# Half of a mixing step folded around the last two weighings, copies and casts moved: a fused attention and low-rank mixer on one NeuronCore

## The chip, the cores and the metric

The kernel runs on one core of a Trainium2 chip. A core has five engines that run their own instruction streams and wait for one another through semaphores: TensorE (PE in the profile, PEld for its weight loads), VectorE (DVE), ScalarE (ACT), GpSimd (POOL) and SyncE (SP). SP here only issues transfers, and POOL and ACT issue some too; sixteen DMA engines carry all of them. The metric is the device time of one execution in microseconds. It was 379.27 us before the change (median of three runs, 377.88 to 379.71).

## The reference

Eight batches (B), eight heads (H), 576 positions (S), head size 64 (D). For each batch and head

```
scores = q k^T / 8 + min(-(cum_i - cum_j), 0)      (j <= i; cum = running sum of max(s, 0))
attn   = softmax(scores) v                          -> x, 576 x 512 per batch
u      = x + (x^T U V)^T                            (U 576 x 32, V 32 x 576: mixing over positions)
out    = u + relu(u W1) W2                          (W1 512 x 2048, W2 2048 x 512)
```

All inputs and the output are float32; inside, the matrix products take bf16.

## The kernel before

**Attention.** A head's scores are computed transposed, key by query, without the masked blocks, in four parts of 448, 448, 448 and 256 columns. `scores` issues each part's matmuls into one of three PSUM banks (tag "s") and ScalarE's exponential (line 323) carries it to a tile `pT`; GpSimd masks the diagonal blocks (`affine_select`, line 338). The bias over `cum` is not added: it rides in four extra rows of q and k, so that the product contains it. `weigh` then multiplies `pT` by v with a column of ones (fifteen matmuls, line 367), and VectorE takes the reciprocal and scales the result into `x_sb`.

**Where q and k come from.** For batches 0 to 2, q and k are read with six positions in a partition (`load_six`, into the space of `hT`) and turned by TensorE (`turn_six`): six transposes into a bank, then copies to `kT` and `qT` (line 303) by VectorE, or ScalarE for some. For batches 3 to 7, `cast(b)` has GpSimd issue two DMAs that convert k and q to bf16 in DRAM (`kq_rows`, line 152); later `turn_batch` has SyncE issue, for each of four head pairs, a transposing DMA of k and one of q (`turn_kq`, line 171), and behind the next pair's two transposes the bias rows of the pair before (`bias_rows`, line 278, from `aug_rows`). SyncE's queue is strictly in program order: a transfer that takes long to issue holds all that follow.

**V.** `fetch_v` has SyncE fetch five tiles of v as float32 into `vf`, and `cast_v` has GpSimd convert them into `v_raw` (line 197). For the first batch these stand in the prologue, two tiles (2 and 3) behind four small copies of bias rows.

**Mixing and layers.** Batches go in pairs (a group). The first batch alone is mixed by `mix_first`, in two halves of 256 columns: a sum over position tiles with `U_cat` (line 438), a copy to `ux0` (ScalarE for the first half, VectorE for the second, line 448), then four parts that add `V_cat`'s product to a transposed x (lines 458, 462) and are copied to `uT` (line 465). `layer1` (line 545, ReLU on ScalarE in line 552) and `layer2` (line 564) follow; `beside` interleaves one group's layers on TensorE with the next group's attention and mixing by written costs, in an order that is fixed when the program is built. So each engine runs a fixed sequence, and an engine that waits holds everything behind it. From the second group on, the mixed x goes to `uT` by transposing DMAs from SyncE (line 520).

**Around the change.** `first_attention` runs batch 0 alone. Between its score parts it places the turns of later head pairs (dictionary `turns`, keyed by head and part) and the weighings of earlier heads (`weighed`); after the loop the last three weighings, the two halves of `mix_first` and the turns of the second batch's first pair follow. `fill` matmuls of zeros stand between score parts. U and V are copied to `U_cat` and `V_cat` by GpSimd in the prologue (`place_UV`, lines 136 to 143). From batch 2 on, `ahead_of(c)` runs at the end of each head of batch c:

```python
if h == (6 if c == 2 else 5) and c + 2 < B and c != 3:
    cast(c + 2)
if 5 <= h and c + 1 < B:
    for t in ((0,), (1, 2), (3, 4))[h - 5]:
        cast_v(c + 1, t)
```

Of the kernel before, what the change touches and what calls it, by code (L numbers as in the profile page):

```python
# [40 lines left out]
def kernel(  # L41
# [92 lines left out]
    def place_UV(bi, engine=nc.gpsimd):  # L134
        r, h = slice(R * bi, R * bi + R), slice(64 * bi, 64 * bi + 64)
        engine.tensor_copy(U_cat[:, 5 * bi : 5 * bi + 4, r], U_f[:, :4])
        engine.tensor_copy(U_cat[h, TAIL, r], U_f[h, 4])

        for r0 in (R * bi, 64 + R * bi):
            rows = slice(r0, r0 + R)  # L140
            V_rows = V_cat[rows].rearrange("r t c -> r (t c)")
            if bi == 0:
                engine.tensor_copy(V_rows[:, :S], V_f[rows])
            else:
                engine.tensor_copy(V_rows[:, 640:], V_f[rows, :512])
                engine.tensor_copy(V_rows[:, 576:640], V_f[rows, 512:])
# [135 lines left out]
    def turn_six(b, hp, which, scalar=0, tag="pv", by_head=False):  # L282
        pb = bank(tag, 2 if tag == "pv" else 3).bitcast(BF16)
        for hh in range(2):
            for t in range(SUB // 2):
                c = RP * (hh * (SUB // 2) + t)
                nc.tensor.transpose(  # L287
                    pb[:, c : c + RP],
                    six[min(b, 1)][which][:, 2 * hp + hh, 2 * D * t : 2 * D * t + 2 * D],
                    identity[:RP, :RP],  # L290
                )
# [4 lines left out]
        for e in range(2):  # L296
            from_ = pb[64 * e : 64 * e + 64, : RP * SUB].rearrange(
                "d (h t p) -> d h p t", h=2, p=RP
            )
            for hs in (slice(0, 1), slice(1, 2)) if by_head else (slice(0, 2),):  # L300
                copies.append((hs, e, from_))
        for hs, e, from_ in sorted(copies, key=lambda one: one[0].start):
            (nc.scalar.copy if e < scalar else nc.vector.tensor_copy)(  # L303
                to[:, hs, :, :, e], from_[:, hs]
            )
# [342 lines left out]
    place_UV(0)  # L648
# [15 lines left out]
    for t in (4, 0, 1):  # L664
        fetch_v(0, t)
    for r in range(AUG):
        direct_rows(0, HP - 1, HP, r)
    for t in (2, 3):
        fetch_v(0, t)
    later = cumulate(2, B, nc.gpsimd)  # L670

    def first_attention():
        turn_six(0, 0, 0)
        turn_six(0, 0, 1, scalar=2)
        ps = bank("s", 3)
# [7 lines left out]
        nc.vector.memset(v_raw[0][:, :, :, D : D + 1], 1.0)  # L683
        for i in (0, 1):
            nc.vector.memset(v_raw[0][:64, TAIL + 5 * i], 0.0)
        clear(ones, 1.0)
        clear(zeros, 0.0)
        nc.sync.dma_start(
            out=kA[1][D : D + 1].rearrange("r n (h s) -> r (n h) s", h=2), in_=ones[:H]
        )  # L690
        for r in range(1, AUG):
            nc.sync.dma_start(
                out=qA[1][D + r : D + r + 1].rearrange("r n (h s) -> r (n h) s", h=2), in_=ones[:H]
            )
        for r in range(AUG):
            direct_rows(1, 0, HP, r)
        load_UV(1)
        nc.sync.dma_start(out=kq[:, :, PAIR:].rearrange("i n c -> (i n) c"), in_=zeros)
        nc.sync.dma_start(
            out=aug[1:4].rearrange("r n s -> n r s"),  # L700
            in_=ones.unsqueeze(1).to_broadcast([BH, 3, S]),
        )
# [44 lines left out]
    def second_at_head(h):  # L747
# [3 lines left out]
        if h == 2:  # L751
            place_UV(1)
# [51 lines left out]
    def ahead_of(c):  # L804


        def at_head(h):
# [6 lines left out]
            if h == (6 if c == 2 else 5) and c + 2 < B and c != 3:  # L814
# [61 lines left out]
```

## Time and profile before

| | |
|---|---|
| median of three runs | 379.27 us (377.88 to 379.71) |
| the profiled execution | 380.7 us, of which 379.0 us from its first to its last instruction |
| mean granted clock of TensorE | 0.990 |
| busy: PE, ACT, DVE, POOL | 364.1, 212.6, 137.9, 108.8 us |
| first batch's exponentials | 10.0 to 24.5 us |
| first matmul of the first layer | 30.46 us |

A row of a timeline gives the start in us from the first instruction, the length in us, the engine (a trailing q marks its queue: an issued transfer), the source line, the operation, output<-input, shapes, and a count; in brackets the engine's idle time before it and what ended that. A row of the chain of waits has start, length and the work. DMA rows in a timeline are the issue, not the transfer. Durations on a line with a count are the whole group's.

### The profile page before, as it was taken

How to read it: one execution, taken by the hardware profiler on the slowest of the kernel's cores; microseconds unless marked ns; L12 is line 12 of the kernel's file. 1: busy time of each engine (PE TensorE's matmuls, PEld its weight loads, DVE VectorE, ACT ScalarE, POOL GpSimd, SP SyncE). 2: the span in 40 equal slices, each digit the busy share in tenths (PEclk: the TensorE clock that was granted, in tenths of full speed). 3: DMA queues.
4: the chain of work that ended last, by engine and by line, in shares of the span. 5: the costliest groups of instructions: out<-in, count | busy, mean ns of one | idle time of the engine just before them, and what ended most of it. 6: DMA issues, size and time to landing. Idle time of an engine off the chain costs nothing.

```text
span 379.0 us, 8262 instructions
## 1 busy us (share of the span) xinstructions
PE 364.1 (96%) x3238; PEld 223.2 (59%) x3259; DVE 137.9 (36%) x308; ACT 212.6 (56%) x496; POOL 108.8 (29%) x169
## 2 busy tenths in 40 slices
PE   6899999999999999969999999999999999999996
PEld 2577784568776456645655446666654445665444
DVE  7968855642224541210234631121224720000221
ACT  5887982479896048956951007888861006773000
POOL 8984983212635022421152001242210000000000
PEclk9999999999999999996999999999999999999999
DMA  7999999798899769996999959600001460000122
GB/s 123 175 184 205 162 202 208 141 207 145 184 209 180 146 136 165 202 202 138 206 170 172 229 131 211 137 4 2 2 29 56 110 148 36 2 0 29 56 83 83
DMA packets 124040, 49.32 MB, mean 130 GB/s; under 512 B 104897, under 2 KB 119201, under 8 KB 124001
## 3 DMA queue, kind: packets, MB, share of 16 engines
q1 hardware_dynamic: 104374, 34.45, 45.0%
q0 software_dynamic: 19056, 14.22, 27.9%
q8 instruction: 25, 0.41, 0.4%
q10 hardware_dynamic: 570, 0.12, 0.2%
q14 instruction: 15, 0.11, 0.1%
HBM read 37.67 MB, written 15.79 MB: 141 GB/s over the span
## 4 chain that ended last, share of the span: by engine, by line
PE 86%; DVE 4%; ACT 3%; DMA 2%; issue 2%; POOL 2%; SPq 1%; ACTq 0%; POOLq 0%; DVEq 0%
PE ps_f L545 32%; PE ps_f L564 31%; PE ps_s L317 10%; PE ps_pv L367 7%; DVE x_sb L516 2%; PE ps_f L512 2%; DMA vf<-in_v_dram 1%; ACT pT L323 1%; PE ps_f L438 1%; PE ps_pv L287 1%; DVE kT L303 1%; ACT x_sb L323 1%; DMA qT<-aug_rows 1%; PE ps_s L309 1%; ACT hT L552 1%
## 5 line engine op out<-in xcount | busy, mean ns | idle before, releaser
L545 PE MATMUL ps_f<-uT,w 128*128 128x384 bf16 (+3 forms) x832 | 160.5, 316 | 0.0
L323 ACT ACTIVATE pT<-ps_s 128x448 bf16<-128x448 f32 x232 | 110.4, 527 | 65.3 <-PE ps_s L317 63.3
L564 PE MATMUL ps_f<-w,hT 128*128 128x512 bf16 (+1 forms) x571 | 136.8, 373 | 1.1
L552 ACT ACTIVATE hT<-ps_f 128x384 bf16<-128x384 f32 (+3 forms) x208 | 102.0, 493 | 47.9 <-PE ps_f L545 46.5
L545 PEld LDWEIGHTS <-w 128*128 128x128 bf16 x832 | 72.9, 98 | 33.5 <-issue 1.6
L338 POOL TENSOR_SCALAR_AFFINE_SELECT pT<-pT 128x640 bf16<-128x640 bf16 x58 | 43.5, 751 | 163.8 <-ACT pT L323 163.7
L564 PEld LDWEIGHTS <-hT 128*128 128x128 bf16 x592 | 54.9, 98 | 57.1 <-issue 3.9
L317 PE MATMUL ps_s<-qT,kT 68*128 68x128 bf16 (+9 forms) x576 | 82.0, 242 | 6.4 <-DMA qT<-aug_rows 3.5
L317 PEld LDWEIGHTS <-kT 68*128 68x128 bf16 (+1 forms) x576 | 46.9, 98 | 34.4 <-issue 9.5
L373 DVE RECIPROCAL rec<-ps_pv 128x5 f32<-128x5 f32 x64 | 12.5, 195 | 126.4 <-PE ps_pv L367 126.1
L575 DVE TENSOR_TENSOR o<-x_sb,ps_f 128x512 f32<-128x512 bf16 (+1 forms) x37 | 24.9, 672 | 86.3 <-PE ps_f L564 85.6
L367 PEld LDWEIGHTS <-pT 128*128 128x128 bf16 x870 | 33.9, 97 | 9.0 <-ACT pT L323 1.0
L367 PE MATMUL ps_pv<-v_raw,pT 128*128 128x65 bf16 x870 | 36.8, 194 | 0.8 <-POOL pT L338 0.5
L379 DVE TENSOR_TENSOR x_sb<-ps_pv,rec 128x320 bf16<-128x320 f32 (+1 forms) x64 | 29.3, 458 | 2.3
L516 DVE TENSOR_TENSOR x_sb<-x_sb,ps_f 128x512 bf16<-128x512 bf16 x32 | 21.2, 686 | 7.4 <-PE ps_f L512 7.1
L197 POOL CAST v_raw<-vf 128x512 bf16<-128x512 f32 (+1 forms) x35 | 21.2, 614 | 8.3 <-DMA vf<-in_v_dram 7.9
L303 DVE COPY kT<-ps_pv 64x576 bf16<-64x576 bf16 x14 | 11.3, 804 | 4.5 <-ACT kT L303 2.8
L309 PE MATMUL ps_s<-uT 128*128 128x512 bf16 (+2 forms) x25 | 9.1, 446 | 1.8 <-DVE uT L105 1.6
L303 DVE COPY qT<-ps_pv 64x576 bf16<-64x576 bf16 x12 | 9.7, 806 | 2.6 <-ACT qT L303 1.9
L512 PE MATMUL ps_f<-ux_sb,V_cat 128*128 128x512 bf16 x27 | 10.2, 379 | 0.4
L287 PEld LDWEIGHTS <-hT 96*128 96x128 bf16 x144 | 8.2, 97 | 3.6 <-issue 0.6
L303 ACT COPY kT<-ps_pv 64x576 bf16<-64x576 bf16 x4 | 3.2, 796 | 9.2 <-PE ps_pv L287 9.2
(104 smaller groups left out, 151.5 us busy)
## 6 DMA issues: line engine op xcount, KB each, us to landing
out_dram<-o SPq DMA_DIRECT2D x31, 256.0 KB
vf<-in_v_dram SPq DMA_DIRECT2D x28, 256.0 KB
w<-in_moe_w_ch_dram POOLq DMA_DIRECT2D x8, 512.0 KB, 8.1
kq_rows<-in_k_dram POOLq DMA_DIRECT2D x5, 576.0 KB, 7.4
kq_rows<-in_q_dram POOLq DMA_DIRECT2D x5, 576.0 KB, 10.3
out_dram<-o SPq DMA_DIRECT2D x10, 128.0 KB
hT<-in_k_dram POOLq DMA_DIRECT2D x4, 288.0 KB, 7.8
hT<-in_q_dram POOLq DMA_DIRECT2D x4, 288.0 KB, 9.5
```

The lines of the kernel that those rows point to most:

```text
L197: (engine or nc.gpsimd).tensor_copy(v_raw[b // 2 % 2][n, 5 * (b % 2) + t, :, :D], vf0[n, t])
L303: (nc.scalar.copy if e < scalar else nc.vector.tensor_copy)(to[:, hs, :, :, e], from_[:, hs])
L317: nc.tensor.matmul(ps[:, col : col + w], lhsT=kt_[:rows, c + kc : c + kc + 128], rhs=qt_[:rows, c + qc : c + qc + w], start=True, stop=True,)
L323: nc.scalar.activation(p[:, at : at + w], ps[:, :w], EXP, scale=scale)
L338: nc.gpsimd.affine_select(out=diagonal, in_=diagonal, compare_op=ALU.is_ge, fill=0.0, base=0, pattern=[[0, 5], [1, 128]], channel_multipli ...
L367: nc.tensor.matmul(pv3[:, it, :], lhsT=p[:, at : at + 128], rhs=vr[:, 5 * bi + j, h, :], start=(j == 0), stop=(j == it),)
L379: nc.vector.tensor_mul(x[:, 5 * bi : 5 * bi + n, h * D : h * D + D], pv3[:, :n, :D], rec[:, :n].unsqueeze(2).to_broadcast([128, n, D]),)
L516: nc.vector.tensor_add(x[:, t, :], x[:, t, :], hp_)
L545: nc.tensor.matmul(f1[:, :cw], lhsT=w1[:, kt, 128 * nf : 128 * nf + 128], rhs=uT[:, kt, c0:c1], start=(kt == 0), stop=(kt == 3),)
L552: nc.scalar.activation(hT[:, nf, c0:c1], f1[:, :cw], RELU)
L564: nc.tensor.matmul(f2[:, :cw], lhsT=hT[:, kt, 128 * t : 128 * t + 128], rhs=w2[:, kt, cs], start=(kt == 0), stop=(kt == 15 and not more),)
L575: nc.vector.tensor_add(o[:, :cw], x_sb[g % 2][:, t, cs], f2[:, :cw])
```

## The change

Six things move; the arithmetic stays the same.

1. U and V for the first batch are placed after the first pair's turns: U's two copies and the first of V's two by ScalarE, V's other copy by GpSimd. `place_UV` is split into `place_U` and `place_V`.
2. v tile 2 is fetched ahead of the last pair's four bias rows; tile 3 stays behind them.
3. The memsets and transfers that stood behind the second pair's k turn (`clear_and_fetch`) now run inside head 0, behind that pair's q turn.
4. Two turns and the weighings move between score parts: six weighings instead of five inside the loop, the first at head 4's third part instead of head 5's second; no fills after head 4.
5. The two last weighings stand inside the first half of `mix_first`. The second batch's first pair is turned behind that half: its k head 0 copied by ScalarE, its q head 0, k head 1 and q head 1 by VectorE, in this order and behind the second half's parts. Before, k was turned ahead of the weighings and copied by ScalarE.
6. The casts of batches 6 and 7 (`cast(c + 2)` for c = 4 and 5) move from head 5 to head 7. That of batch 4 stays at head 6.

```diff
-    place_UV(0)
...
-    for t in (4, 0, 1):
+    for t in (4, 0, 1, 2):
         fetch_v(0, t)
     for r in range(AUG):
         direct_rows(0, HP - 1, HP, r)
-    for t in (2, 3):
-        fetch_v(0, t)
+    fetch_v(0, 3)
...
         turn_six(0, 0, 1, scalar=2)
+        place_U(0, nc.scalar.copy)
+        place_V(0, (nc.scalar.copy, nc.gpsimd.tensor_copy))
...
-        turns = {(0, 1): (1, 1, "f"), (1, 3): (2, 0, "f"), (2, 1): (2, 1, "pv"), (2, 3): (3, 0, "pv"), (3, 3): (3, 1, "f")}
-        weighed = {(5, 1): 1, (6, 0): 1, (6, 2): 1, (7, 0): 1, (7, 2): 1}
+        turns = {(0, 1): (1, 1, "f"), (1, 3): (2, 0, "f"), (2, 2): (2, 1, "pv"), (3, 0): (3, 0, "pv"), (3, 3): (3, 1, "f")}
+        weighed = {(4, 2): 1, (5, 1): 1, (5, 3): 1, (6, 1): 1, (6, 3): 1, (7, 1): 1}
+        halves = [mix_first(dt) for dt in (0, 2)]
...
-            fills = 0 if h in (0, 1, H - 1) else 320 if h < HP else 448
+            fills = 0 if h < 2 or h > HP else 320 if h < HP else 448
...
+                if (h, n) == (0, 2):
+                    clear_and_fetch()
...
-        halves = [mix_first(dt) for dt in (0, 2)]
-        turn_six(1, 0, 0, scalar=2, tag="s")
+        one, two = halves
+        next(one)
         weigh(*done.pop(0))
-        next(halves[0])
+        next(one)
+        next(one)
         weigh(*done.pop(0))
-        weigh(*done.pop(0))
-        for _ in halves[0]:
+        for _ in one:
             pass
-        for _ in halves[1]:
+        next(two)
+        on_scalar, on_vector = [nc.scalar.copy] * 2, [nc.vector.tensor_copy] * 2
+        heads = slice(0, 1), slice(1, 2)
+        k_copies = turned(
+            1, 0, 0, "s", [(heads[0], on_scalar), (heads[1], on_vector)]
+        )
+        for copy in k_copies[:2]:
+            copy()
+        for _ in two:
             pass
-        turn_six(1, 0, 1, tag="s", by_head=True)
+        q_copies = turned(1, 0, 1, "s", [(hs, on_vector) for hs in heads])
+        for copy in q_copies[:2] + k_copies[2:] + q_copies[2:]:
+            copy()
...
-            if h == (6 if c == 2 else 5) and c + 2 < B and c != 3:
+            if h == (6 if c == 2 else 7) and c + 2 < B and c != 3:
                 cast(c + 2)
```

`turned` is the body of `turn_six` that issues the six transposes and gives back the copies as functions, so that the caller places them.

More of the change, by code (lines that the diff above doesn't have):

```diff
@@ L2 @@
 from contextlib import ExitStack
+from functools import partial
 from itertools import islice
@@ L278, in bias_rows, with turn_six, turned @@
             nc.sync.dma_start(out=to[n % RING][D:KA, : 2 * S], in_=aug_v[r, n])
-    def turn_six(b, hp, which, scalar=0, tag="pv", by_head=False):
+    def turn_six(b, hp, which, scalar=0, tag="pv"):
+        engines = [nc.scalar.copy if e < scalar else nc.vector.tensor_copy for e in range(2)]
+        for one in turned(b, hp, which, tag, [(slice(0, 2), engines)]):
+            one()
+    def turned(b, hp, which, tag, copiers):
         pb = bank(tag, 2 if tag == "pv" else 3).bitcast(BF16)
@@ L295, in turn_six @@
         copies = []
[L296 to L305, printed above, removed]
+        for hs, engines in copiers:
+            for e in range(2):
+                from_ = pb[64 * e : 64 * e + 64, : RP * SUB].rearrange(
+                    "d (h t p) -> d h p t", h=2, p=RP
+                )
+                copies.append(partial(engines[e], to[:, hs, :, :, e], from_[:, hs]))
+        return copies
     def fill(ps, w):
@@ L751, in second_at_head @@
         if h == 2:
-            place_UV(1)
+            place_U(1)
+            place_V(1)
         if 1 <= h <= 4:
```

53 lines of the change are left out of this document (28 added, 25 removed).

## The prediction

> **What bounds the kernel now.** I read the page first, for the busy shares and the granted clock; then the chain of waits, which showed a transfer ending TensorE's wait near 168 us; then tables by stretch, to price that place; then timelines of single engines and the DMA view, to see who holds whom.
>
> ```profile
> span 379.0 us, 8262 instructions
> PE 364.1 (96%) x3238; PEld 223.2 (59%) x3259; DVE 137.9 (36%) x308; ACT 212.6 (56%) x496; POOL 108.8 (29%) x169
> PEclk9999999999999999996999999999999999999999
> ```
>
> TensorE is busy 96% of the span: a change pays only where TensorE waits or runs slowly. One slice of forty has a low clock, the nineteenth (from 170.6 us). Two stretches of the same program, TensorE's work beside the attentions of batches 4, 5 and of batches 6, 7, can be laid on each other:
>
> ```profile
> 140.68:164.01 23.33, 23.33 (x258) 16.08 (x257) 4.11 (x12) 21.31 (x52) 9.27 (x14) 1.00 1.16 180
> 164.01:188.62 24.61, 21.11 (x190) 13.44 (x188) 4.10 (x13) 16.64 (x40) 4.76 (x7) 0.86 0.99 176
> 231.74:255.08 23.34, 23.34 (x260) 16.09 (x257) 4.12 (x12) 21.32 (x52) 6.33 (x10) 1.00 0.60 102
> 255.08:273.37 18.29, 18.26 (x189) 12.32 (x188) 4.10 (x13) 15.96 (x40) 4.76 (x7) 1.00 0.01 2
> 167.60:171.10 3.50, 0.05 (x1) 0.01 (x1) 0.00 (x0) 0.25 (x1) 0.00 (x0) 0.82 0.90 193
> 171.10:176.80 5.70, 5.68 (x27) 3.23 (x28) 0.00 (x0) 3.83 (x8) 0.75 (x1) 0.51 0.85 164
> ```
>
> (Start and end, length, then busy time of PE, PEld, DVE, ACT, POOL; last the granted clock, DMA share and rate.) The first halves agree within 0.01 us. The second halves hold the same work, 190 and 189 matmuls, yet take 24.61 and 18.29 us: 6.32 us are lost between 164 and 189. The last two rows say how: 3.5 us of an idle TensorE, then 5.7 us at a clock of 0.51, which costs another 2.8. The timeline of TensorE names the wait (first row), and with the offset of 91.07 us (255.08 less 164.01) the later stretch tells when batch 5's heads 0 and 2 would start if nothing were late:
>
> ```profile
> 171.12 0.53 PE L317 MATMUL ps_s<-qT,kT 68*128 68x64 bf16 x4 [3.48 <-DMA qT<-aug_rows]
> 258.55 0.36 PE L317 MATMUL ps_s<-qT,kT 68*128 68x64 bf16 x4
> 264.20 0.47 PE L317 MATMUL ps_s<-qT,kT 68*128 68x192 bf16 x6
> ```
>
> Head 0 wants its rows at 167.48 and got them at 171.12; head 2 wants those of the next pair at 173.13. The rows come from SyncE's queue, in order:
>
> ```profile
> 158.26 1.95 SPq L171 DMA_TRANSPOSE qT<-kq_rows  x1
> 160.30 5.66 SPq L171 DMA_TRANSPOSE kT<-kq_rows  x1
> 166.02 1.68 SPq L171 DMA_TRANSPOSE qT<-kq_rows  x1
> 168.32 0.26 SPq L278 DMA_DIRECT2D qT<-aug_rows  x1
> ...
> 185.86 2.15 SPq L171 DMA_TRANSPOSE kT<-kq_rows  x1
> 190.06 0.27 SPq L278 DMA_DIRECT2D qT<-aug_rows  x1
> 191.72 1.35 SPq L171 DMA_TRANSPOSE qT<-kq_rows  x1
> 193.96 1.88 SPq L171 DMA_TRANSPOSE kT<-kq_rows  x1
> 195.89 5.89 SPq L171 DMA_TRANSPOSE qT<-kq_rows  x1
> 212.71 3.90 SPq L520 DMA_TRANSPOSE uT<-x_sb  x3
> ```
>
> Most transposes take 1.35 to 2.15 us to issue here; two take 5.66 and 5.89. What they share is a cast issued on POOL shortly before (first and third row; the second is head 7's):
>
> ```profile
> 157.44 0.73 POOL L152 DMA_DIRECT2D kq_rows<-in_k_dram  x1
> 164.55 1.29 POOL L197 CAST v_raw<-vf 128x512 bf16<-128x512 f32 x2
> 193.19 0.73 POOL L152 DMA_DIRECT2D kq_rows<-in_k_dram  x1
> ```
>
> The held transposes begin 2.86 and 2.70 us after their cast and end 8.52 and 8.59 us after it. The DMA view of 160.3 to 166 us (packets, MB, share of the 16 engines), and as a control the row of the SyncE queue from 188 to 193 us, show what holds them:
>
> ```profile
> q0 software_dynamic: 890, 1.01, 103.7%
> q1 hardware_dynamic: 498, 0.12, 16.5%
> ...
> q1 hardware_dynamic: 4083, 1.03, 94.8%
> ```
>
> The cast takes the engines; SyncE's queue moves 0.12 MB in 5.7 us, against 1.03 MB in 5 us without a cast.
>
> **Term 1: the two casts.** They move from head 5 to head 7 of batches 4 and 5. For batch 4, head 7's mask ends at 164.55, where the V casts now stand, so the first cast issues there, 7.1 us later than before. The k transpose of 160.30 then flows. In batch 6 the q bias copy issues 4.20 us after the same transpose (185.86 to 190.06), 3.35 if that transpose takes 1.3 instead of 2.15; from 159.7 to 160.3 (the transpose of 158.26 done in 1.4 us, or in 1.95 as now) this gives 163.1 to 164.5. The old copy issued at 168.32 and was used at 171.12, 2.80 us later; so head 0 has its rows at 165.9 to 167.3, against 167.48. The idle time goes, and with it the slow clock: 6.32 us, the full difference of the two stretches. Bounds: nothing at all, or the whole 6.32.
>
> What is late next is the second pair. In batch 6 its q transpose starts 5.86 us after the same k transpose (185.86 to 191.72), 5.0 with the quicker first one: here at 164.7 to 166.1, most likely 165.3. Of the quoted cases, those that started about 0.8 us after a cast (158.26, 193.96) still got out in under 2 us; those at 2.7 and 2.86 did not. The cast is now at 164.55, so this one starts 0.15 to 1.6 us behind it. I take it that it passes; head 2 needs the rows only at 173.13. That is the closest call of this forecast.
>
> POOL's two cast issues (2 x 0.73) now delay V casts of tiles 3 and 4 to about 167.3; batch 5's first weighing is a head behind its start (two heads take 5.65 us, 258.55 to 264.20), at 170.3, so this costs nothing. The cast of batch 7 moves likewise to about 201 and holds SyncE's transposes until some 8.6 us later; the mixing's transposes come at 212.71. No cost; if that cast lasted 4 us longer, the third group's first layer would still find its tiles, which its first matmul needs at 228.53:
>
> ```profile
> 228.53 0.49 PE L545 MATMUL ps_f<-uT,w 128*128 128x384 bf16 x2
> ```
>
> **Term 2: the first 32 us.** Rows of ACT, DVE, PE and POOL, and a weighing in the chain of waits (20.78):
>
> ```profile
> 2.98 0.67 ACT L636 COPY kT<-key_ones 64x576 f32<-64x576 f32 x1
> 10.00 3.28 ACT L323 ACTIVATE pT<-ps_s 128x448 bf16<-128x448 f32 x8 [1.50 <-PE ps_s L317]
> 13.77 5.21 ACT L323 ACTIVATE pT<-ps_s 128x448 bf16<-128x448 f32 x12 [0.49 <-PE ps_s L317]
> 11.09 1.39 POOL L143 CAST V_cat<-w 32x576 bf16<-32x576 f32 x2
> 16.96 0.62 POOL L197 CAST v_raw<-vf 128x512 bf16<-128x512 f32 x1 [0.35 <-DMA vf<-in_v_dram]
> 18.89 0.62 POOL L197 CAST v_raw<-vf 128x512 bf16<-128x512 f32 x1
> 20.78 0.46 PE ps_pv L367 x15
> 24.38 1.62 ACT L303 COPY kT<-ps_s 64x576 bf16<-64x576 bf16 x2
> 28.41 0.42 DVE L448 CAST ux<-ps_f 128x256 bf16<-128x256 f32 x1 [1.29 <-PE ps_f L438]
> 30.46 1.58 PE L545 MATMUL ps_f<-uT,w 128*128 128x256 bf16 x12
> 30.66 1.98 DVE L303 COPY qT<-ps_s 64x288 bf16<-64x288 bf16 x4 [0.25 <-PE ps_s L287]
> ```
>
> U and V on ScalarE: three copies. One of 576 columns takes 0.67; by columns the two of U are nearer 0.3 and 0.2, together 1.2 us, at most 2.0. ScalarE idles 1.50 us before its first exponential: hidden, or 0.5 late. POOL loses those three (one of the two V copies is half of 1.39, the U copies some 0.5 by columns), and V tile 2 is fetched ahead of four small row copies, so that POOL's 0.35 us wait for it ends: together 1.5 us, of which I count 1.0, since POOL's masks still wait for the exponentials. The last V cast comes at 17.9 instead of 18.89. But the first weighing, which waits for it, also moves up by three score parts, about 1.15 us of exponentials (eight parts take 3.28). The memsets behind the second pair's copies end the 0.49 us gap. These roughly cancel: the exponentials end at 24.5 to 24.8, as now (the k copies follow them at 24.38).
>
> Then the 1.62 us of k copies no longer stand between the last exponential and the mixing's cast. Now the k copies end at 26.00, the mixing's cast follows, and the second half's cast comes 2.41 us later (28.41), the first layer 2.05 after that (30.46). With the last weighing (0.46) inside that stretch it is 2.87 and 2.05 from an end of the exponentials at 24.5 to 24.8: the first layer starts at 29.4 to 29.7, a gain of 0.75 to 1.05. Part is given back: six half copies on VectorE (0.48 to 0.5 each, 3 us) now hold two of the three score banks until 32.4 to 32.8, and the second attention's second and third parts wait for them, 0.3 to 0.5 us. Net gain 0.6; bounds 1.3 (nothing given back, the gap saved too) and a loss of 1.0 (the early weighing stalls TensorE for the cast without cover, and the copies come late).
>
> **Sum.** The profiled execution took 380.7 us (379.0 span), 1.43 above the median of the runs. 380.7 - 6.3 - 0.6 = 373.8; against the median, 379.27 - 6.9 = 372.4.
>
> [...]
>
> **Rivals.**
> *The wait moves to head 2.* If the second pair's q transpose starts more than about 1.2 us after the cast, it is caught until 173.1 and its rows arrive, by the same 5.15 us from held transpose (165.97) to matmul less the transpose between (1.7), at 176.5: 3.4 us idle, plus the clock, and all of term 1 is back. 379.27 - 0.6 = 378.7. Caught in part, 374 to 377. For it: the range of 0.15 to 1.6 us straddles the mark. Against: its likeliest value is 0.75, and both transposes at 0.8 us got through.
>
> *Slower: head 0's own rows are caught.* If the two transposes and two bias copies from 160.3 took over 5.5 us, the bias rows would fall into the new cast and wait until 173.1, arriving near 176: 8.5 us idle and 3 of slow clock, 11.5 in place of 6.3. 379.27 + 5.2 - 0.6 = 383.9. Against: from 185.86 to 190.33 the same four took 4.47 us.
>
> *The cast is not the cause.* Then the held transpose has another reason and stays. The engines' sharing is the point: if both queues got half, the 5.66 us would be 2.6 by doubling, and only 1.3 us of the wait could go with the cast: 379.27 - 0.6 - 1.3 = 377.4. The 16.5% against 103.7% speaks clearly against it. [...]
>
> **How the numbers follow.** Full gain 0.55 (370.8 to 374.0: the bounds of term 2 and 0.3 for jitter); caught in part 0.18; wait moved to head 2 0.14; caught at head 0 0.07; not the cast 0.04; term 2 lost with term 1 won 0.02, near 374. The range reaches to 378.0, which takes in the part caught, the third rival and some of the second pair's case; 0.17 is left out. About 0.5% (1.9 us) is what a measurement of this kernel can tell from no change: faster holds the first two, the last, and parts of the others, 0.77; same 0.15; slower 0.08.
>
> **What would show it.** Right: no wait of TensorE on bias rows between 160 and 185, the clock at 1.00 there, a transpose of over 5 us that begins about 3 us after a cast, but later (pair 3 of batch 5), and 164-to-189's work in 18.3 us. The first layer's first matmul at 29.4 to 29.8. Wrong: a wait at head 2 of batch 5 or a slow slice near 170; a gap on TensorE over 1 us before the first weighing; ScalarE's first exponential after 10.3.

## The result, and the profile after

The changed kernel takes 374.93 us (median of four, 374.51 to 382.31) against 379.49 for the kernel before, measured beside it. The ratio is 0.988, with a 95% interval of 0.984 to 0.992: 1.2% faster, some 4.5 us. Runs as long as the one of 382.31 are left out of the ratios, here and below; what such a run may hold is in the first experiment. The profiled execution took 374.79 us (span 373.1), 5.9 less than the one before (380.7). The forecast was 372.4 in a range of 370.8 to 378.0: the range held, the figure was 2.5 us too low.

From the page of the changed kernel, the span, the busy time and share of each engine, and the granted clock in 40 slices:

```profile
span 373.1 us, 8277 instructions
PE 363.2 (97%) x3255; PEld 222.8 (60%) x3255; DVE 139.2 (37%) x310; ACT 212.2 (57%) x499; POOL 108.2 (29%) x166
PEclk9999999999999999999999999999999999999999
```

The low slice near 170 us is gone. The same two stretches as in the prediction, now of batches 4 and 5 in the changed kernel (start and end, length, busy PE, PEld, DVE, ACT, POOL, then clock, DMA share, GB/s):

```profile
141.09:164.42 23.33, 23.33 (x259) 16.08 (x257) 4.12 (x12) 21.31 (x52) 7.83 (x12) 1.00 1.08 191
164.42:182.71 18.29, 18.26 (x190) 12.33 (x188) 4.11 (x13) 15.96 (x40) 6.25 (x9) 1.00 0.98 157
```

The second stretch takes 18.29 us where it took 24.61: the 6.32 us of term 1, to the hundredth. But it starts 0.41 us later than before (164.42 against 164.01). So 6.32 - 0.41 = 5.91, the difference of the profiled executions. All that happened lies in these two numbers: from 183 us to the end the offset stays at 5.91, so the cast of batch 7, moved as well, cost nothing.

SyncE's and GpSimd's rows around the moved cast (timeline of the changed kernel), and under them the DMA view of the held transpose, 166.76 to 172.4 us, with the two rows of that view from 160 to 180 us that give the casts' times from issue to landing:

```profile
159.59 1.39 SPq L174 DMA_TRANSPOSE qT<-kq_rows  x1
161.60 0.26 SPq L281 DMA_DIRECT2D qT<-aug_rows  x1
...
165.09 0.29 SPq L281 DMA_DIRECT2D qT<-aug_rows  x1
...
166.76 5.64 SPq L174 DMA_TRANSPOSE qT<-kq_rows  x1
164.96 0.74 POOL L155 DMA_DIRECT2D kq_rows<-in_k_dram  x1
```

```profile
q0 software_dynamic: 771, 0.87, 92.8%
q1 hardware_dynamic: 538, 0.14, 18.1%
...
kq_rows<-in_k_dram POOLq DMA_DIRECT2D x1, 576.0 KB, 6.9
kq_rows<-in_q_dram POOLq DMA_DIRECT2D x1, 576.0 KB, 9.9
```

Head 0's bias rows are issued at 161.60, 6.7 us earlier than before, and the second pair's at 165.09, 0.13 us behind the cast of 164.96. A transpose is still held for 5.64 us, but it is the last pair's, which nobody asks for soon. The shares are near those of the case before (103.7 and 16.5%): 93% for the cast, 18% for SyncE's queue.

The first 32 us (timeline of the changed kernel; ACT, PE, POOL and SP rows):

```profile
10.73 6.56 ACT L329 ACTIVATE pT<-ps_s 128x448 bf16<-128x448 f32 x16 [0.66 <-PE ps_s L323]
20.43 0.38 ACT L329 ACTIVATE pT<-ps_s 128x256 bf16<-128x256 f32 x1 [1.09 <-PE ps_s L323]
19.94 0.34 PE L373 MATMUL ps_pv<-v_raw,pT 128*128 128x65 bf16 x6 [1.21 <-POOL v_raw L200]
30.54 1.58 PE L551 MATMUL ps_f<-uT,w 128*128 128x256 bf16 x12
32.76 0.35 PE L323 MATMUL ps_s<-qT,kT 68*128 68x320 bf16 x2 [0.23 <-DVE kT L760]
17.34 0.62 POOL L200 CAST v_raw<-vf 128x512 bf16<-128x512 f32 x1 [0.61 <-DMA vf<-in_v_dram]
19.27 0.62 POOL L200 CAST v_raw<-vf 128x512 bf16<-128x512 f32 x1
7.44 4.16 SPq L194 DMA_DIRECT2D vf<-in_v_dram  x4
16.00 0.46 SPq L194 DMA_DIRECT2D vf<-in_v_dram  x1
```

The first weighing, moved up, meets a last V cast at 19.27 instead of the forecast 17.9: TensorE stalls 1.21 us in the middle of that weighing, and ScalarE behind it 1.09. The first layer starts at 30.54, where it started at 30.46, not at 29.4 to 29.7.

### The profile page after: what moved, and what is told of

The parts are those of the page before. It is cut to its first block, busy times and chain, and to the rows that moved or that the text cites. A ratio compares the mean times of both kernels' runs of the same rounds, so it can differ in the third digit from the quotient of the medians.

```text
span 373.1 us, 8277 instructions
## 1 busy us (share of the span) xinstructions
PE 363.2 (97%) x3255; PEld 222.8 (60%) x3255; DVE 139.2 (37%) x310; ACT 212.2 (57%) x499; POOL 108.2 (29%) x166
## 4 chain that ended last, share of the span: by engine, by line
PE 87%; DVE 3%; DMA 3%; ACT 3%; POOL 2%; SPq 1%; issue 1%; ACTq 0%; POOLq 0%; DVEq 0%
PE ps_f L570 32%; PE ps_f L551 31%; PE ps_s L323 10%; PE ps_pv L373 8%; DMA vf<-in_v_dram 2%; DVE x_sb L522 2%; PE ps_f L518 2%; ACT pT L329 1%; PE ps_f L444 1%; PE ps_pv L296 1%; ACT x_sb L329 1%; DMA sel<-in_s_dram 1%; POOL pT L344 1%; ACT hT L558 1%; SPq L194 1%
## 5 line engine op out<-in xcount | busy, mean ns | idle before, releaser
L551 PE MATMUL ps_f<-uT,w 128*128 128x384 bf16 (+3 forms) x832 | 158.4, 313 | 0.0
L570 PE MATMUL ps_f<-w,hT 128*128 128x512 bf16 (+1 forms) x592 | 140.4, 373 | 0.4
L344 POOL TENSOR_SCALAR_AFFINE_SELECT pT<-pT 128x640 bf16<-128x640 bf16 x58 | 43.9, 756 | 158.0 <-ACT pT L329 157.5
L323 PE MATMUL ps_s<-qT,kT 68*128 68x128 bf16 (+9 forms) x576 | 80.8, 239 | 1.6 <-ACT x_sb L329 0.5
L323 PEld LDWEIGHTS <-kT 68*128 68x128 bf16 (+1 forms) x576 | 46.1, 97 | 28.0 <-issue 3.9
```

What stands on the lines that cost most here:

```text
L323: nc.tensor.matmul(ps[:, col : col + w], lhsT=kt_[:rows, c + kc : c + kc + 128], rhs=qt_[:rows, c + qc : c + qc + w], start=True, stop=True,)
L344: nc.gpsimd.affine_select(out=diagonal, in_=diagonal, compare_op=ALU.is_ge, fill=0.0, base=0, pattern=[[0, 5], [1, 128]], channel_multipli ...
L551: nc.tensor.matmul(f1[:, :cw], lhsT=w1[:, kt, 128 * nf : 128 * nf + 128], rhs=uT[:, kt, c0:c1], start=(kt == 0), stop=(kt == 3),)
L570: nc.tensor.matmul(f2[:, :cw], lhsT=hT[:, kt, 128 * t : 128 * t + 128], rhs=w2[:, kt, cs], start=(kt == 0), stop=(kt == 15 and not more),)
```

## The experiments

In the expectations, "the changed kernel" is the kernel above. Diffs are against it unless the kernel before is named.

**Each half alone.** The first kernel is the kernel before with the two casts moved, the second is the changed kernel with the casts moved back.

```diff
# e1_casts, against the kernel before
-            if h == (6 if c == 2 else 5) and c + 2 < B and c != 3:
+            if h == (6 if c == 2 else 7) and c + 2 < B and c != 3:
# e2_first, against the changed kernel
-            if h == (6 if c == 2 else 7) and c + 2 < B and c != 3:
+            if h == (6 if c == 2 else 5) and c + 2 < B and c != 3:
```

> The kernel before with only the two casts of batches 6 and 7 moved from head 5 to head 7; the first mixing as before. Theory (the cast alone held the transpose, and the whole gain of the change is here): a profiled time 6.3 us below that of the kernel before, so 373.0 against a median of 379.3; no wait of TensorE on bias rows between 160 and 185 us; the second half of the stretch (164 to 189 us) takes 18.3 us instead of 24.6. Rival (the restructured first mixing has a part in it, by shifting when batch 5's rows are asked for): more than 375.0, with a TensorE wait left near 168.

> The changed kernel with the two casts back at head 5: the first mixing's change alone. As predicted (-0.6 us): 378.7. Theory after the trace of the changed kernel, where the offset to the kernel before is +0.4 us at 140 us: the first 140 us are no shorter, 379.3 to 379.9, with a stall of TensorE of about 1.2 us at the first weighing, on the cast of the last V tile. If the late start of that one profile (first exponential 10.73 instead of 10.00) was chance and not the change, the first exponential here is back at 10.0 to 10.3 and the first layer starts 0.7 earlier than 30.54, at about 29.8.

Measured: the casts alone 374.75 us, ratio 0.987 (0.983 to 0.992), the whole gain of the change; the first mixing alone 379.68, ratio 1.001 (0.998 to 1.004), no difference that can be measured. The gain is the casts'. The 373.0 expected of the first is missed by 1.7 us; that is the step from the profiled execution to the median, taken up below.

The profiled execution of the casts alone was not like its median: it took 379.89 us. Its timeline (PE, SP and POOL rows) shows the prediction's first rival at work:

```profile
177.20 0.53 PE L317 MATMUL ps_s<-qT,kT 68*128 68x64 bf16 x4 [3.24 <-DMA qT<-aug_rows]
165.06 1.29 SPq L171 DMA_TRANSPOSE qT<-kq_rows  x1
166.92 0.39 SPq L278 DMA_DIRECT2D qT<-aug_rows  x1
172.02 5.06 SPq L171 DMA_TRANSPOSE qT<-kq_rows  x1
165.10 0.74 POOL L152 DMA_DIRECT2D kq_rows<-in_k_dram  x1
```

Head 0 ran on time; TensorE waited 3.24 us at head 2, for the second pair's bias rows. These were issued at 166.92, 1.8 us behind the cast, and used at 177.20, 10.3 us later. In the changed kernel's profile the same copy stands 0.13 us behind its cast, and nothing waits. The prediction watched the q transpose ahead of these copies (it called it the second pair's; it is the third's, and the second pair's bias copies stand behind it). Its issue passed, at 165.06 in 1.3 us. Its transfer did not: by the updates of its semaphore in the trace it landed at 176.36, 11.3 us after its issue, and the last of the bias copies behind it, of 9 KB each, at 176.95. In the changed kernel the same transpose was issued at 163.23, 1.7 us ahead of the cast instead of 0.04, and landed at 166.72. A short issue is no landing: the q transpose of 158.26 in the kernel before, which the prediction counts among those that got out in under 2 us, landed at 167.69.

The first mixing's profile has the held transpose back, and shows where its own time is set (timeline; PE, POOL, SP and ACT rows):

```profile
170.51 0.36 PE L323 MATMUL ps_s<-qT,kT 68*128 68x64 bf16 x4 [2.45 <-DMA qT<-aug_rows]
157.86 0.74 POOL L155 DMA_DIRECT2D kq_rows<-in_k_dram  x1
160.67 5.28 SPq L174 DMA_TRANSPOSE qT<-kq_rows  x1
9.64 3.28 ACT L329 ACTIVATE pT<-ps_s 128x448 bf16<-128x448 f32 x8
20.04 0.34 PE L373 MATMUL ps_pv<-v_raw,pT 128*128 128x65 bf16 x6 [1.19 <-POOL v_raw L200]
30.55 1.58 PE L551 MATMUL ps_f<-uT,w 128*128 128x256 bf16 x12
```

I had put part of the late first layer down to a late start (first exponential at 10.73). Here the first exponential is at 9.64 and the first layer still at 30.55: that theory fell. The weighing waits for the last V cast, whatever the start.

**The clock.** Twelve idle matmuls fill TensorE's wait in the kernel before.

```diff
# e3_clock, against the kernel before, in attention(b, at_head)
             p = next_p()
+            if (b, h) == (5, 0):
+                ps = bank("s", 3)
+                for _ in range(12):
+                    nc.tensor.matmul(ps, lhsT=w1[:, 0, :128], rhs=w1[:, 0, :512], start=True, stop=True)
             quanta = scores(HP * b + h // 2, h % 2, p)
```

> The kernel before with twelve idle matmuls of 512 columns (2.6 us at full clock) put ahead of batch 5's first scores, where TensorE waits 3.48 us for the bias rows. The wait for the rows stays. Theory (the slow clock of 5.7 us follows from the idle time and costs 2.8 us of the 6.3): the granted clock stays at 1.00 near 171, the wait shrinks by 2.6 us on the page but the first score still starts at about 171.1, and the time is 2.8 us below the kernel before: 376.5. Rival (the clock drops there for another reason): no gain, 379.3, and a slice with 0.5 stays.

Measured: 378.19 us, ratio 0.998 (0.994 to 1.001). The trace did as expected:

```profile
167.43 2.75 PE L405 MATMUL ps_s<-w 128*128 128x512 bf16 x12
171.21 0.36 PE L317 MATMUL ps_s<-qT,kT 68*128 68x64 bf16 x4 [1.03 <-DMA qT<-aug_rows]
```

The fills take 2.75 us (2.6 was an estimate). The score starts at 171.21 as before (171.12), the clock stays at 1.00, and the rest of the program runs 2.6 us earlier than in the trace before. So the slow clock does follow from the idle time and cost about what was taken for it, in that execution. The median moved by 1.2 only. One reason is in the runs: of 29 runs of the kernel before in this series the five shortest (376.8 to 377.1) had a mean granted clock of 1.00 over the whole run, the others 0.986 to 0.995: not every execution loses it. Another is in this trace: the last exponentials and the last output's sum come 2.6 us earlier than before (373.19 against 375.80), but the span ends only 1.5 us earlier, for a reason that the trace does not show. A third may be that the fills cost their 2.75 us where the rows come early; that was not traced.

In the kernel before the granted clock stood at 0.50 from 169.85 to 176.68, 6.83 us; with the casts alone from 177.12 to 180.54 and in the next experiment from 177.25 to 180.67, 3.42 us each, half as long. So stretches are cut here into pieces of 3.41 us, in step with the places where the granted clock changed (where it did not change nearby, in step with the clock's first entry in that trace). The falls at 169.85 and 177.25 lie 48 and 50 such pieces behind the first entries in their traces (6.01 and 6.59 us). Shown are two rows each of the kernel before, of the first mixing alone, of the next experiment, and of the prologue of one further below, with the cast at head 0 (same columns as above):

```profile
166.44:169.85 3.41, 1.21 (x13) 0.56 (x10) 0.69 (x2) 0.66 (x2) 0.00 (x0) 1.00 1.03 220
169.85:173.27 3.42, 2.15 (x11) 1.35 (x12) 0.00 (x0) 1.48 (x3) 0.00 (x0) 0.50 0.91 183
```

```profile
166.45:169.87 3.42, 1.61 (x20) 0.95 (x20) 0.69 (x2) 1.06 (x3) 0.00 (x0) 1.00 1.29 196
169.87:173.28 3.41, 2.77 (x25) 1.94 (x26) 0.00 (x0) 2.32 (x7) 0.75 (x1) 1.00 1.03 182
```

```profile
173.84:177.25 3.41, 1.10 (x12) 0.69 (x11) 0.00 (x0) 1.18 (x5) 0.00 (x0) 1.00 1.06 168
177.25:180.67 3.42, 3.42 (x26) 2.13 (x25) 0.91 (x3) 1.70 (x5) 0.75 (x1) 0.50 0.45 105
```

```profile
5.64:9.05 3.41, 1.71 (x18) 0.79 (x17) 2.51 (x12) 1.94 (x5) 3.29 (x7) 1.00 0.79 125
9.05:12.47 3.42, 3.42 (x23) 2.26 (x24) 1.83 (x3) 1.48 (x3) 2.31 (x4) 0.50 1.12 217
```

Near 170 us, a piece in which TensorE was busy 1.21 us, or 1.10, is followed by one at half clock; a piece with 1.61 is not. This is no threshold for the whole program: in the prologue a piece with 1.71 us was followed by half clock too (last two rows), and why is open. The wait of 2.45 us of the first mixing alone fell across two pieces and cost only itself; the next experiment's 2.31 us fell into one and cost half of 3.42 more.

**The cast at head 6.**

```diff
# e4_head6
-            if h == (6 if c == 2 else 7) and c + 2 < B and c != 3:
+            if h == 6 and c + 2 < B and c != 3:
```

> The changed kernel with the two casts at head 6 instead of head 7, so the cast issues near 161.4 us, 2.9 us earlier. Theory (a cast takes the DMA engines from about 2.8 us after its issue until 8.5 us after it): the transpose that starts at about 164 us, one of the second pair's of batch 5, is held until 169.9 instead of one of pair 3; head 0's rows (copied from 161.6 to 165.4 in the changed kernel) pass or are just caught. The second pair's rows then arrive at about 171.7 to 173, against their use at about 173.1 less nothing: no loss if head 0's rows pass (374.9), 1 to 4 us if the q bias copy of head 0 is caught (376 to 379). Rival (only the order of issue matters, not the time): 374.9 with no transpose held over 2.5 us.

Measured: 379.76 us median of ten (375.89 to 384.73), ratio 0.995 (0.990 to 0.999). The timeline (PE, SP, POOL):

```profile
176.34 0.36 PE L323 MATMUL ps_s<-qT,kT 68*128 68x64 bf16 x4 [2.31 <-DMA qT<-aug_rows]
165.61 5.24 SPq L174 DMA_TRANSPOSE qT<-kq_rows  x1
161.27 0.74 POOL L155 DMA_DIRECT2D kq_rows<-in_k_dram  x1
```

Head 0's rows passed, and the third pair's q transpose was held until 170.85, a microsecond later than expected. The second pair's bias rows followed it (171.41) and were used at 176.34: TensorE waited 2.31 us at head 2, plus the slow piece. I had allowed 1.8 to 3.1 us from the end of the hold to their arrival and called this case no loss; it took 5.5, because the held transpose itself landed only at 175.85 by its semaphore. The held issue moved with the cast: it ended 8.5, 9.6 and 7.4 us after casts of 157.44 (before), 161.27 and 164.96 (the changed kernel), which no rival about the order of issue explains. In the other traces with a whole cast at head 5 or 7 the last held issue ended 7.6 to 12.0 us after it.

**Half a cast, and a cast in small pieces.** k's part at head 5 and q's at head 7; then, in the kernel before, casts cut into 144 elements a piece instead of 576.

```diff
# e7_split
-    def cast(b):
-        for i, src in enumerate((k, q)):
+    def cast(b, which=(0, 1)):
+        for i in which:
+            src = (k, q)[i]
...
-            if h == (6 if c == 2 else 7) and c + 2 < B and c != 3:
-                cast(c + 2)
+            if h == 6 and c == 2:
+                cast(c + 2)
+            if h in (5, 7) and c in (4, 5):
+                cast(c + 2, (int(h == 7),))
# e8_small, against the kernel before
-                out=kq[i, HP * b : HP * b + HP, :PAIR].rearrange("n (r c) -> r n c", r=128),
+                out=kq[i, HP * b : HP * b + HP, :PAIR].rearrange("n (r c) -> r n c", r=512 if b > 5 else 128),
...
-                .rearrange("n (r c) -> r n c", r=128),
+                .rearrange("n (r c) -> r n c", r=512 if b > 5 else 128),
```

> The changed kernel with each of the two casts split: k's part at head 5, q's part at head 7. Theory (the hold is as long as the cast's transfer, so half the bytes hold half as long): a transpose of batch 5 issued near 160 is held about 2.5 to 3 us instead of 5.3 to 5.7, head 0's rows come at about 167 to 168.5 against their use at 167.3, and TensorE waits 0 to 1.5 us without a slow clock: 375 to 376.5. Rival (any cast holds a transpose for the same 5 us): a wait of 2.5 to 3.5 us and 378 to 380.

> The kernel before with the casts of batches 6 and 7 cut into pieces a quarter as long (144 elements instead of 576), still at head 5. Theory A (the DMA engines take turns by packet, so the share of a queue goes with the size of its packets): the held transpose is let through in about half the time, 2.5 to 3 us, while the cast itself lasts longer; TensorE's wait at 168 falls below 1.5 us and the time to 375 to 377. Theory B (the casting queue is served before SyncE's until it is done, whatever the packets' size): the transpose is held for as long as the cast lasts, 5.7 us or more, and the time is 379.5 or above.

Measured: 377.63 us for the split cast (ratio 0.995, 0.991 to 0.998) and 383.01 for the small pieces (one run at 376.84, three at 382.8 to 383.5; no interval). The split's timeline, from an execution of 381.09 us (SP, POOL, PE rows):

```profile
159.50 4.20 SPq L175 DMA_TRANSPOSE kT<-kq_rows  x1
157.60 0.74 POOL L156 DMA_DIRECT2D kq_rows<-in_k_dram  x1
164.71 0.74 POOL L156 DMA_DIRECT2D kq_rows<-in_q_dram  x1
171.39 0.53 PE L324 MATMUL ps_s<-qT,kT 68*128 68x64 bf16 x4 [3.58 <-DMA qT<-aug_rows]
```

Half the bytes hold the transpose until 6.1 us after the cast instead of 7.4 to 12.0, so the hold does shrink with the bytes, but not to half: it was 4.2 us long and not 2.5 to 3. The half cast itself landed 6.3 us after its issue. That moved head 0's bias copies to 165.20 and 165.72, behind the second half's cast of 164.71, and they were caught there until 171.4: 6.7 us after that cast's issue. No transpose was under way ahead of them then (the last had landed at 166.92), so here the copies themselves were held. This is the prediction's slower rival, met with half a cast.

The small pieces: the DMA view from 161.62 to 165.56, while a transpose is held, and from the timeline the score of head 0.

```profile
q0 software_dynamic: 1784, 0.51, 123.8%
q1 hardware_dynamic: 697, 0.17, 33.6%
```

```profile
173.01 0.53 PE L317 MATMUL ps_s<-qT,kT 68*128 68x64 bf16 x4 [5.29 <-DMA qT<-aug_rows]
```

With packets a quarter as long (1784 for 0.51 MB, against 771 for 0.87) SyncE's queue moved 177 packets a microsecond (697 in 3.94 us) against 87 in the kernel before (498 in 5.7) and 95 in the changed kernel (538 in 5.64), and the transpose's issue got through in 3.94 us instead of 5.66. So far theory A: with the other queue's packets shorter, SyncE's queue moved more of its own. But the cast itself was now under way until 14.0 us after its second issue instead of 8.8 in the kernel before, the next transposes were slow too, and TensorE waited 5.29 us. Theory A has the shorter hold, theory B the time in three of the four runs; the one of 376.84 was not profiled. That the engines take turns by packet was theory A's assumption and is not shown: for one packet of SyncE's queue the cast's moved 1.4 in the changed kernel (771 to 538) and 2.6 here (1784 to 697). Nor do the shares, 92.8 to 18.1% there and 123.8 to 33.6% here, show the equal halves by which the prediction priced its third rival.

**One step later still.** Batch 6's cast goes to head 0 of batch 5, when all of batch 5's rows are on their way; first on the changed kernel, then on the kernel before, which prices the first mixing without a collision.

```diff
# e6_head0; e10_old_half is the same edit on the kernel before
-            if h == 0 and c == 4:
+            if h == 0 and c in (4, 5):
                 cast(c + 1)
+            if h == 0 and c == 4:
                 for t in range(5):
                     fetch_v(c + 1, t)
...
-            if h == (6 if c == 2 else 7) and c + 2 < B and c != 3:
+            if h == (6 if c == 2 else 7) and c in (2, 5):
```

> The changed kernel with the cast of batch 6 one step later still, at head 0 of batch 5, and that of batch 7 at head 7 of batch 5 as in the change. Theory (the only thing still exposed is what of batch 5's rows follows the cast on SyncE's queue; in the one look at the casts alone the second pair's bias rows, issued 1.3 to 1.8 us after the cast, landed about 10 us late and TensorE waited 3.24 us at head 2): no transpose of batch 5 over 2.6 us, no wait of TensorE on bias rows in any profile, 374.5 us median with a narrow spread, none of the timed runs over 377. Rival (the spread has another cause): runs near 380 to 382 remain among those at 374.

> The kernel before, with its old first mixing, and only the casts moved: batch 6's to head 0 of batch 5, batch 7's to head 7. This prices the new first mixing without the collision that scatters the times. If the new first mixing is a gain of 0.6 us as predicted: 375.2. If it costs the 0.4 us by which the changed kernel's ScalarE lies behind at 140 us: 374.2. No run over 376.5 either way.

> The changed kernel itself once more, for the spread of its times: three of four runs lay at 374.5 to 375.1 and one at 382.3. Theory (the second pair's rows are caught by the cast in some executions and not in others, by a margin of about a microsecond): two groups, most at 374.2 to 375.5 and some at 379 to 383, with few between. Rival (the one long run was a disturbance): all runs at 374 to 376.

The last of these is the changed kernel once more, for its spread. Measured, medians and all runs: cast at head 0 374.61 (374.29 to 375.84, six runs); the same with the old first mixing 374.28 (374.09 to 375.72, six); the changed kernel again 374.74 (373.95 to 375.44 for five, and one of 379.93). From the timeline with the cast at head 0, the last pair's q transpose, no longer held, and the cast:

```profile
169.20 2.33 SPq L174 DMA_TRANSPOSE qT<-kq_rows  x1
171.60 0.73 POOL L155 DMA_DIRECT2D kq_rows<-in_k_dram  x1
```

Of the changed kernel's ten runs two lie at 379.9 and above, of the casts' alone one of seven. With the cast one step later no run lies above 375.9, in 22 runs of four kernels. That fits the margin which the trace of the casts alone shows lost (the third pair's q transpose 0.04 us ahead of the cast instead of 1.7); for the long runs that were not profiled it stays argued. The median gains nothing from it, 0.3 us being within what these runs tell apart.

The old first mixing is 0.3 us ahead of the new one here: on the side of a small cost, not settled.

**The last V tile.** Fetched with the others, and cast ahead of the next batch's load; then the same with the cast at head 0; then also with the last pair's q rows turned a head later.

```diff
# e5_tile3; e9_both adds the edit of e6_head0
-    for t in (4, 0, 1, 2):
+    for t in (4, 0, 1, 2, 3):
         fetch_v(0, t)
...
-    fetch_v(0, 3)
...
-            for t in {1: (4, 0), 2: (1, 2), 3: (3,)}.get(h, ()):
+            for t in {1: (4, 0), 2: (1, 2, 3)}.get(h, ()):
# e11_turn, against e9_both
-        turns = {(0, 1): (1, 1, "f"), (1, 3): (2, 0, "f"), (2, 2): (2, 1, "pv"), (3, 0): (3, 0, "pv"), (3, 3): (3, 1, "f")}
+        turns = {(0, 1): (1, 1, "f"), (1, 3): (2, 0, "f"), (2, 2): (2, 1, "pv"), (3, 0): (3, 0, "pv"), (4, 3): (3, 1, "f")}
```

> The changed kernel with the last V tile (tile 3) fetched together with the other four, ahead of the four small row copies, and its cast put ahead of the next batch's load on POOL. Theory (the end of the first 32 us is set by the last V tile's cast, which stands at 19.27 to 19.44 us in three profiles whose first exponential was at 9.64, 10.05 and 10.73): the cast ends at 18.6 to 18.9 instead of 19.9, TensorE's stall at the first weighing falls from 1.1 to 1.2 us to 0.5 or less, the first layer starts 0.6 to 1.1 us earlier than 30.55, at about 29.6, and the time is 374.0. Rival (the early weighings delay the exponentials whatever the cast does, since TensorE is full): the first layer stays at 30.4 or later, 374.9.

> The changed kernel with both mends: batch 6's cast at head 0 of batch 5, and the last V tile fetched with the others and cast ahead of the load. Theory (the two are independent): the first layer at about 29.96 as with the V tile alone, no wait on bias rows, a median 0.5 to 0.6 us under that of the cast's mend alone: 374.0, and no run over 376. Rival (the earlier V tile's 0.6 us is lost again, or brings the collision back): 374.6 or more, or runs near 380 and above.

> Both mends and one more: the last pair's q rows are turned one head later (behind head 4's scores instead of head 3's), so that VectorE's two copies of it (1.6 us) no longer stand ahead of the first weighing's normalisation. Theory (TensorE's 0.90 us stall at 21.0 with the early V tile is that normalisation, which came late behind those copies): the stall goes, the first layer starts at 29.1 to 29.4 instead of 29.96, and the median is 373.4. Rival (the copies are now late for head 6, which uses them): TensorE waits as long there on the q rows and the time is 374.0 or more.

Measured: the V tile alone 374.2 to 374.7 in five runs, but 379.7 to 383.0 in five others; with the cast at head 0 374.46 (374.01 to 375.88); with the turn moved too 374.74 (374.57 to 375.65). The timeline of the V tile alone (POOL, PE):

```profile
17.46 0.62 POOL L200 CAST v_raw<-vf 128x512 bf16<-128x512 f32 x1 [0.90 <-DMA vf<-in_v_dram]
21.00 0.61 PE L373 MATMUL ps_pv<-v_raw,pT 128*128 128x65 bf16 x15 [0.90 <-DVE x_sb L385]
29.96 1.58 PE L551 MATMUL ps_f<-uT,w 128*128 128x256 bf16 x12
```

The cast comes 1.8 us earlier, the stall at the first weighing is gone, and the first layer starts at 29.96. A new stall of 0.90 us at the third weighing, on VectorE's scaling behind the turns' copies, takes back half. Moving a turn left a stall of 0.59 us on VectorE at 21.45, with the first layer at 30.18. That the five long runs are the collision again, brought on by heads that come earlier than their rows, is argued from its absence with the cast at head 0; none of them was profiled.

No version beats the changed kernel's median by more than the runs can tell. The old first mixing with the cast at head 0 is the shortest, and does without the rest of the change.

## Why the prediction was right, and where not

*Bound and place.* Right: TensorE's wait on batch 5's bias rows, held by a transpose, held by a cast. With the casts alone moved the gain is whole, with the casts back it is gone, and the rival that the cast is not the cause fell with these runs.

*Term 1, 6.32 us.* Right to the hundredth in the profiled execution. Head 0's q rows were issued at 161.60, ahead of the predicted 163.1 to 164.5, since all four transposes ran in 1.3 to 1.9 us (the first took 3.37 before).

*The second pair, "the closest call".* Right in naming it, right in its price (3.4 us idle at 176.5 forecast; 3.24 at 177.20 in the trace of the casts alone), wrong in what to watch. It took a transpose as through when its issue was short; what decided was when the transfer landed, 11.3 us after its issue in the trace of the casts alone. It placed the q transpose 0.15 to 1.6 us behind the cast and took it that it passes; where it passed, it stood 1.1 to 1.7 us ahead, and 0.04 us ahead it was caught, with the bias copies 1.3 to 1.8 us behind the cast. That the changed kernel mostly escapes is in part luck: a margin that the prediction did not count on. Nor was it one case or the other: the kernel with the casts alone moved has a trace with them caught at 379.89 us, and a median of 374.75 that leaves no room for that.

*Term 2, a gain of 0.6.* Wrong; this step failed. In the traces, first layer's start and ScalarE's lag at 120 us against the kernel before (starts of the same exponential):

```
first mixing   kernel           first exp.  last V cast  first layer  lag at 120 us
old            before             10.00       18.89        30.46         0
old            e1_casts            9.64       19.43        31.00        +0.54
old            e3_clock            9.77       18.83        30.41        -0.05
old            e10_old_half        9.85       18.74        30.31        -0.14
old            e8_small           10.03       18.52        30.52        +0.07
new            changed            10.73       19.27        30.54        +0.41
new            e12_again          10.12       18.82        29.99        -0.16
new            e2_first            9.64       19.38        30.55        +0.41
new            e4_head6           10.05       19.44        30.62        +0.48
new            e6_head0           11.38       19.58        31.62        +1.47
new            e7_split           10.02       19.11        30.29        +0.16
new, V early   e5_tile3            9.68       17.46        29.96        -0.18
new, V early   e9_both            10.44       18.19        30.26        +0.12
new, V early   e11_turn           10.20       17.88        30.18        +0.05
```

The new mixing's first layer starts where the old one's does (middle value 30.55, against 30.31 to 31.00). The mis-sized term is "the last V cast comes at 17.9 instead of 18.89": it comes at 18.8 to 19.6. I had taken GpSimd's saved copies as the limit. But the wait for tile 2, which was to end, grew from 0.35 to 0.61 us in the changed kernel, and was 1.41 with the first mixing alone and 0 to 0.55 in the four other traces. And tile 3's fetch, put behind tile 2's and the four row copies, now issues at 14.1 to 16.0 instead of about 12.7. In the changed kernel it landed at 19.14 instead of 17.77, by its semaphore; in four of the six traces with this order its cast waited for it, 0.34 to 1.04 us, as GpSimd's timeline of the changed kernel's second trace shows:

```profile
18.82 0.61 POOL L200 CAST v_raw<-vf 128x512 bf16<-128x512 f32 x1 [0.59 <-DMA vf<-in_v_dram]
```

The order of the fetches is not all of it: with the casts alone, in the old order, tile 3's cast waited 0.58 us too. So the earlier weighing stalls, which the prediction held as the bound of a loss ("stalls TensorE for the cast without cover"); a gap on TensorE of over 1 us there and a first exponential after 10.3 were among its signs of being wrong, and both came (1.21 us and 10.73). The other links held: from the end of the exponentials (25.74) to the first layer it takes 4.80 us, against 5.95 before, a gain of 1.15 for the forecast 0.75 to 1.05; and what is given back behind the first layer, which the prediction put down to the half copies on VectorE, is 0.33 (a lag of 0.08 at the first layer, 0.41 at 120 us), for 0.3 to 0.5; TensorE's row at 32.76 shows 0.23 of it as a wait for one of these copies. U and V on ScalarE were hidden: ScalarE still idles 0.66 us ahead of its first exponential.

*From the profiled execution to the median.* This step cost more: "against the median, 379.27 - 6.9". The profiled execution stood 1.43 above the median because it held the full wait and two slow pieces, which other executions hold in part: its mean clock was 0.990, that of the 376.8 to 377.1 us runs 1.00. (What those lost was not traced; only their clocks are on record.) After the change the runs without a collision vary little: 374.79 profiled, 374.93 median. The forecast for the median should have been the sum for the profiled execution, 373.8. Of the 2.5 us, 1.0 is term 2 (-0.6 forecast, +0.41 measured) and 1.4 this shift; 0.1 is left. That the range held is in part luck: 374.93 lies outside the band given to the full gain (370.8 to 374.0) and inside that of a part caught (374 to 377), which is not what the profiled execution shows. Its lower end counts term 2 twice: 372.4 already holds the 0.6, so a bound of 1.3 with 0.3 for jitter ends at 371.4 and not 370.8; nothing hangs on it.

*The clock.* Right that the slow clock goes with the idle time: with the fills the rest ran 2.6 us earlier in that trace, of the 2.8 counted. The length of the wait alone does not tell: 2.31 us brought the clock down, 2.45 did not. Nor need the piece before the fall be idle: TensorE worked 1.10 and 1.21 us in two that brought it down.

## To carry to other kernels

Here a casting transfer between DRAM tensors (two parts of 576 KB, landed 6.9 and 9.9 us after their issue in the changed kernel) held transfers of another queue until 7.4 to 12.0 us after its first issue. So place such a transfer behind the issue of everything that is wanted within its time, and look at when the transfers land, not only at how long they take to issue. If the wait that a change removes varies from run to run, forecast the time after from the profiled sum and not as the median less the gain. When work is moved up, price the last of its inputs through every queue that input passes.

## What the runs showed of the hardware

A bias copy of 9 KB that followed a cast of 1.18 MB by 1.8 us was used 10.3 us after its issue, though both queues moved data in that time (77.4% and 43.9% from 167.4 to 177.1 us); the transpose ahead of it on its queue took 1.3 us to issue and 11.3 us to land. The granted clock stood at half for 6.83 us in the kernel before and for 3.42 us near 179 us in two traces of the experiments. Near 170 us it fell after a piece in which TensorE was busy 1.21 us or less and stayed after one with 1.61, so that a wait of 2.31 us cost some 1.7 us more (half of 3.42), one of 3.48 us some 2.6 (from the trace with the fills), and one of 2.45 us nothing. And with one and the same first mixing the first layer started anywhere from 29.99 to 31.62 us, the latest with a piece at half clock from 9.05 us; under a microsecond, single traces of this prologue prove little.
